# A new order for the first steps of a retention-and-feed-forward kernel: loads, conversions and steps rearranged, some sums tied to program order

## The chip, the cores and the metric

The kernel runs on one core of a Trainium2 chip. The metric is the time of one execution on the device in microseconds (us); lower is better.

## The reference

A retention block is followed by a feed-forward block with a gate. In the first, 4 batches of 8 heads run over 768 positions with 64 channels:

```
state = gamma[h] * state + outer(k[t], v[t])
y[t]  = (1 / sqrt(64)) * q[t] @ state
```

In the second, the heads are laid side by side, so that x has 3072 rows of 512:

```
h   = x @ w_in                            # 512 x 2048
g   = h * (1 / (1 + exp(-1.702 * h)))
out = g @ w_out                           # 2048 x 512
```

All is float32. The two weights reach the kernel as 64-bit numbers, of which it makes 32-bit ones itself.

## The kernel before

**Blocks.** The 3072 rows of x are cut into blocks of 512 (m = 0 to 5). A block is made from four steps; a step (j = 0 to 23) treats 64 positions of two batches for all heads. For a step, q, k and v are loaded (L140), q and k are turned by TensorE into `pt` (turn, L250) and copied out by ACT (turned, L261), TensorE makes the scores `pa` (L289), DVE multiplies them with the mask (masked, L318), and a second half of the step multiplies scores, old state and v (L297, L306, L312). A step's first half is written `stepJ` in the order below and its second half `step-J`; `step1-0` is the first half of 1 with the second half of 0. decay (L272 on ACT, L274 on POOL) weighs k for the state; aged (L357, L359), updated (L366, L368), state (L325) and x (L347, L349) finish a step on ACT, POOL and DVE.

**Weights.** The 16 pairs of weight pieces w0 to w15 come in two loads each (a and b, 512 KB, L180) into three raw buffers used in turn, `RAWS`. The conversion is: abs on ACT (L207), half on DVE (L211, L212, L213), rest on DVE (L217, L218, L222). The pair w0 is converted in two pieces, 0a and 0b.

**Products.** In m = 0 the first layer is plain: `up0.th.p` (L414) takes half the rows (th) and a pair p of weight pieces; `gate` (L393) follows on ACT. In m = 1 the first layer uses seven products for eight (`seven`, L491). From m = 2 on `up` does so (L562), with sums of X (`sums_x`, L530 to L533, on POOL) and of the weights (`sums_w1`). The second layer is `down` for m = 0 and 1 (L799) with sums of gates (`sums_g`, L546 to L548, DVE; `sums_g_late`, L552, POOL) and of w_out (`sums_w2`, L537 to L539; `sums_w2_t3`, L542), and for m = 2 to 5 `down49` (L666), a two-level form which streams weight sums from DRAM through `ring` (`stream`, L635, on POOL) and adds up outputs in `put` (L687 on DVE, L692 to L696 on POOL).

**What sets the order.** TensorE runs in program order. The steps 0 to 7, the conversions and the first layer of blocks 0 and 1 are called from one list of names, written by hand; `pin` (`tc.keep_in_program_order`) holds the instructions of the other engines in that order too, on each engine and each load queue. After the list `ordered` is false, and a scheduler places the instructions that aren't held one by one. Loads are issued from the queues of SP, ACT and POOL, each in its own order.

Of the kernel before, what the change touches and what calls it, by code (L numbers as in the profile page):

```python
# [28 lines left out]
def kernel(  # L29
# [95 lines left out]
    def load(j, what="qkv"):  # L125
# [20 lines left out]
        if j < NEW:  # L146
            if "q" in what:
                plain("q", q, "q_sq", 2)
            if "k" in what:
                plain("kn", k, "k_sq" if j in (0, 1, 4, 5) else "o", 2, pool if j else act)  # L150
# [31 lines left out]
    class Narrow:  # L182
# [26 lines left out]
        def half(self):  # L209
            m, mu, hi = self.m, self.mu, self.hi  # L210
            pin(dve.tensor_scalar(m, m, F64_MOST * 2.0 ** 16, F64_LEAST * 2.0 ** 16, op0=ALU.min, op1=ALU.max))  # L211
            pin(dve.tensor_scalar(mu, mu, 3, None, op0=ALU.logical_shift_left))  # L212
            pin(dve.scalar_tensor_tensor(hi, hi, 0x80000000, mu, op0=ALU.bitwise_and, op1=ALU.bitwise_or))  # L213

        def rest(self):
            m, mu, lo, hi = self.m, self.mu, self.lo, self.hi
            pin(dve.tensor_scalar(mu, hi, 0xFF800000, None, op0=ALU.bitwise_and))  # L217
            pin(dve.scalar_tensor_tensor(lo.bitcast(F32), lo, 2.0 ** -52, m, op0=ALU.mult, op1=ALU.mult))  # L218
            a, b = lo.bitcast(F32), hi.bitcast(F32)
# [42 lines left out]

    def decay(j):
# [5 lines left out]
        if j < NEW:  # L269

            for h in range(H):
                pin(act.activation(KD[j][:, h], x[:, h % HP * 2 + h // HP], AF.Copy, scale=cold[:, H + h:H + h + 1]))  # L272
        else:
            pin(pool.tensor_mul(KD[j].rearrange("p (i s) d -> p i s d", i=2), x.rearrange("p (i s) d -> p i s d", i=2),  # L274
                                cold[:, None, H:H + HP, None].to_broadcast([P, 2, HP, D])))
# [94 lines left out]
    def step(j, f=None):  # L370
        attend(j, f)
        if j is not None:
            masked(j)
            if j > 2 * CB:
                decay(j)
# [145 lines left out]
    def sums_w1(p):  # L521
        t, q1 = w1(p)
        w = [t[:, q1:q1 + 2, s] for s in range(7)]
        pool.tensor_add(w[4], w[2], w[3])
        pool.tensor_sub(w[6], w[0], w[2])
        pool.tensor_sub(w[5], w[4], w[0])
        pool.tensor_sub(w[2], w[1], w[5])

    def sums_x():
        tc.keep_in_program_order(pool.tensor_sub(X[:, 4], X[:, 2], X[:, 0]))  # L530
        pool.tensor_sub(X[:, 6], X[:, 3], X[:, 2])
        pool.tensor_sub(X[:, 5], X[:, 3], X[:, 4])
        pool.tensor_sub(X[:, 2], X[:, 1], X[:, 5])  # L533
# [7 lines left out]
    def sums_w2_t3(p):  # L541
        dve.tensor_sub(W2[:, 6, p:p + 2, :], W2[:, 5, p:p + 2, :], W2[:, 0, p:p + 2, :])  # L542
# [7 lines left out]
    def sums_g_late(m, p):  # L550
        a = [g(m, p, s) for s in range(2)]
        tc.keep_in_program_order(pool.tensor_sub(a[1], a[1], a[0]))  # L552
# [79 lines left out]
    def stream(ring, i):  # L632

        c = ring[:, i % 2 * 3:i % 2 * 3 + 3]
        pool.dma_start(c, W2D[i])  # L635
# [7 lines left out]
    def down49(m, ring, comps):  # L643
# [39 lines left out]
        def put(th, e, half, y, a):  # L683
# [8 lines left out]
            eng.tensor_add(c[:, 1:3], c[:, 1:3], c[:, 0:1].to_broadcast([P, 2, P]))  # L692
            eng.tensor_add(c[:, 3], c[:, 3], c[:, 2])
            eng.tensor_add(c[:, 0:5:4], c[:, 2:4], c[:, 4:5].to_broadcast([P, 2, P]))
            eng.tensor_add(c[:, 2:4], c[:, 0:4:3], c[:, 5:7])
            (act if last else pool).dma_start(rows[th, e], c[:, 1:5].rearrange("p (b f) e -> p b (f e)", b=2))  # L696
# [39 lines left out]
        for i in range(7):  # L736
            for half in range(2):
                def unit(i=i, half=half):
# [11 lines left out]
                    products(acc[x, half], pairs[i][half], i not in (2, 3))  # L750
                    then(i, half, acc[x, half])
                    if half == 0 and i < 6:
                        pairs[i + 1] = derive(i + 1)
                    if half == 1:
                        if i + 2 < 7:
                            comps[i + 2] = stream(ring, i + 2)
# [5 lines left out]
    def down(m):  # L762
# [61 lines left out]
        for n, d in order:  # L824
            key, sa, sb, new, last, then = P_[n]
            def unit(key=key, sa=sa, sb=sb, new=new, last=last, d=d, then=then, n=n):
# [3 lines left out]
                if n == 4 and d == 3:  # L830
# [27 lines left out]

    def rows():
# [9 lines left out]
    def lay_rowd():  # L869

        for o in range(2):
            pin(act.activation(rowd[HALF[o]], products["rows"][HALF[o], o:H:2, :], AF.Copy))

# [11 lines left out]
    def halves_anew():  # L885
# [18 lines left out]
        "warm": keep_warm}  # L904
# [17 lines left out]
    for name, i in [("0a", 0), ("0b", 1)] + [(str(p), 2 * p) for p in range(1, NFF)]:  # L922
        n = Narrow(i)
        works |= {"abs" + name: n.start, "half" + name: n.half, "rest" + name: n.rest}
# [19 lines left out]
    for name in """  # L944
        k0 table q0 warm turn0 w0b rows warm k1 abs0b q1 turned0 step0 v0 w0a half0b mask k2 turn1 causal rest0b
        masked0 decay0 v1 decay1 abs0a half0a step-0 updated0 turned1 q2 step1 rowd whole w2b turn2 w2a x0 k3
        aged1 masked1 turned2 v2 rest0a abs2 q3 step-1 updated1 state1 decay2 aged2 step2 q4 x1 half2 decay3 w3b
        w3a up0.0.0 masked2 turn3 k4 step-2 v3 q5 rest2 k5 gate0.0.0 turned3 updated2 state2 step3 up0.0.2
        masked3 abs3 half3 x2 rest3 turn4 w1b step-3 aged3 gate0.0.2 turned4 state3 w1a w5b updated3 v5 decay4
        abs1 x3 turn5 half1 up0.0.3 turned5 up0.1.2 step4 aged4 w5a rest1 v4 gate0.0.3 decay5 w6a masked4  # L950
        gate0.1.2 abs5 w6b step5-4 half5 rest5 up0.0.1 updated4 abs6 state4 gate0.0.1 w4b
        up0.1.1 half6 aged5 w4a up0.0.5 rest6 masked5 up0.1.5 gate0.1.1 x4 gate0.0.5 abs4 step-5 w8b w8a
        half4 gate0.1.5 state5 updated5 anew q6 up0.1.6 x5 rest4 gate0.1.6 abs8 v6 decay6 aged6 up0.0.6 w7b w7a half8
        turn6 gate0.0.6 up0.1.0 abs7 seven_4.2 seven_6.2 half7 gate0.1.0 w9b w9a up0.1.4 q7 gate0.1.4 step6 masked6 rest7 up0.0.4 v7
        gate0.0.4 seven_52.2 turn7 up0.1.3 gate0.1.3 step7-6 seven_4.0 masked7 updated6 decay7 aged7 abs9 state6 x6 up0.0.7 rest8 seven_w.0 gate0.0.7
# [10 lines left out]
    for m in range(NB):  # L966
# [31 lines left out]
        for n, unit in enumerate(down(m) if m < 2 else down49(m, *ring)):  # L998
# [3 lines left out]
            if m == 0 and NP <= n < 3 * NP // 2:  # L1002
                sums_w2_t3(2 * (n - NP))
            if m == 1 and n % 8 == 3:
                sums_w1(n // 4)
# [4 lines left out]
            if 0 < m < NB - 1 and n == (23 if m == 1 else 11):  # L1010
# [47 lines left out]
```

## Time and profile before

| what | us |
|---|---|
| median of three runs | 661.61 |
| lowest, highest | 657.32, 662.9 |
| the profiled execution | 662.24 |
| its span | 660.5 |
| TensorE busy | 642.2 |
| DVE busy | 453.9 |
| POOL busy | 198.8 |
| ACT busy | 159.0 |

The page gives busy time by engine, and a row of digits for each engine in which one digit stands for the busy tenths of a fortieth of the span, 16.5 us. PE is TensorE, PEld its weight loads, DVE the vector engine, ACT the scalar engine, POOL GpSimd, SP the queue that issues most loads. In the lists of waits a line has the waiting engine with tile and line, the releaser, and then total, number and longest in us. In timelines a line has start, duration, engine, line, operation, output and inputs, and in brackets the idle time before it with what ended it.

### The profile page before, as it was taken

The page shows a single profiled execution, that of the slowest core. Times are in us where ns is not written, and L with a number is a line of the kernel's source. Part 1 is how long each engine was busy: PE and PEld are TensorE (multiplying, and loading weights), DVE is VectorE, ACT ScalarE, POOL GpSimd, SP SyncE. Part 2 cuts the span into 40 slices and gives each one's busy share as a digit, 9 for nine tenths or more (in the row PEclk, how much of TensorE's full clock was granted, in tenths as well). Part 3 has the DMA queues.
Part 4 walks back from the last instruction along what each step waited for, and adds up shares of the span by engine and source line. Part 5 has one row for each costly group of instructions (what it writes and reads, how often), then busy time and mean ns, then how long its engine had stood idle before and what let it go on. Part 6 is the DMA issues. An engine that isn't in the chain of part 4 may idle for free.

```text
span 660.5 us, 15291 instructions
## 1 busy us (share of the span) xinstructions
PE 642.2 (97%) x6390; PEld 580.2 (88%) x6390; DVE 453.9 (69%) x645; ACT 159.0 (24%) x306; POOL 198.8 (30%) x225
## 2 busy tenths in 40 slices
PE   6789999999999999999999999999999999999997
PEld 3778888888788888889999888999888999988997
DVE  3699989999936973556984445995354995254965
ACT  4674233551000000333100233010233110233110
POOL 6400311310379217000536400445600255500000
PEclk9989999999999999999999999999999999999999
DMA  9995549763233556262485832386742252602142
GB/s 176 193 274 173 152 104 241 172 163 60 49 82 135 137 149 153 58 248 96 118 199 134 279 57 97 86 223 135 225 118 97 66 154 104 235 21 96 55 154 96
DMA packets 148149, 91.86 MB, mean 139 GB/s; under 512 B 131600, under 2 KB 134416, under 8 KB 147056
## 3 DMA queue, kind: packets, MB, share of 16 engines
q1 hardware_dynamic: 135856, 45.19, 29.8%
q0 software_dynamic: 9888, 44.46, 20.6%
q10 hardware_dynamic: 2336, 1.25, 0.6%
q8 instruction: 50, 0.82, 0.5%
q14 instruction: 19, 0.16, 0.1%
HBM read 72.89 MB, written 15.47 MB: 134 GB/s over the span
## 4 chain that ended last, share of the span: by engine, by line
PE 89%; DVE 4%; DMA 4%; SPq 1%; issue 1%; ACT 0%; DVEq 0%
PE pq L666 27%; PE px L562 17%; PE pd L799 13%; PE py L562 13%; PE ph L491 7%; PE ph L414 5%; PE pa L289 2%; PE py L312 2%; PE pa L297 2%; PE py L306 2%; DMA W<-in_moe_w_in_dram 1%; DMA W<-in_moe_w_out_dram 1%; DMA q_in<-in_q_dram 1%; PE pt L250 1%; SPq L140 1%
## 5 line engine op out<-in xcount | busy, mean ns | idle before, releaser
L635 POOL DMA_DIRECT2D ring<-W2D x28 | 15.4, 551 | 227.7 <-PE px L562 118.3
L666 PE MATMUL pq<-W,G 128*128 128x128 f32 x672 | 80.2, 276 | 0.0
L666 PEld LDWEIGHTS pq<-W,G 128*128 128x128 f32 x672 | 77.6, 192 | 1.3 <-issue 0.7
L666 PE MATMUL pq<-ring,own 128*128 128x128 f32 x448 | 60.1, 276 | 1.3 <-issue 1.3
L562 PE MATMUL px<-X,W1A 128*128 128x256 f32 x256 | 59.8, 379 | 0.0
L562 PE MATMUL px<-X,W1B 128*128 128x256 f32 x256 | 59.8, 379 | 0.0
L666 PEld LDWEIGHTS pq<-ring,own 128*128 128x128 f32 x448 | 54.5, 192 | 0.4
L562 PEld LDWEIGHTS px<-X,W1B 128*128 128x128 f32 x256 | 48.5, 190 | 6.7
L562 PEld LDWEIGHTS px<-X,W1A 128*128 128x128 f32 x256 | 48.4, 190 | 6.5
L393 ACT ACTIVATE G<-G 128x512 f32<-128x512 f32 x60 | 37.4, 628 | 54.7 <-DVE G L572 33.4
L799 PE MATMUL pd<-W,G 128*128 128x256 f32 x224 | 49.6, 381 | 0.0
L799 PEld LDWEIGHTS pd<-W,G 128*128 128x128 f32 x224 | 42.2, 190 | 5.9
L562 PE MATMUL py<-X,W1A 128*128 128x256 f32 x192 | 45.4, 379 | 0.0
L562 PE MATMUL py<-X,W1B 128*128 128x256 f32 x192 | 45.4, 379 | 0.0
L562 PEld LDWEIGHTS py<-X,W1A 128*128 128x128 f32 x192 | 36.5, 190 | 5.0
L562 PEld LDWEIGHTS py<-X,W1B 128*128 128x128 f32 x192 | 36.5, 190 | 5.0
L580 DVE TENSOR_TENSOR t<-py,u 128x512 f32<-128x512 f32 x16 | 11.1, 692 | 32.3 <-PE py L562 32.3
L569 ACT ACTIVATE p<-px 128x512 f32<-128x512 f32 x16 | 9.6, 597 | 96.0 <-PE px L562 96.0
L414 PE MATMUL ph<-X,W1A 128*128 128x256 f32 x128 | 30.6, 397 | 0.9 <-DVE X L347 0.9
L594 DVE TENSOR_TENSOR G<-G 128x512 f32<-128x512 f32 (+2 forms) x24 | 12.3, 513 | 25.7 <-ACT G L393 25.7
L666 PE MATMUL pq<-ring,G 128*128 128x128 f32 x224 | 29.6, 275 | 0.0
L666 PE MATMUL pq<-W,own 128*128 128x128 f32 x224 | 29.6, 275 | 0.0
(237 smaller groups left out, 1226.0 us busy)
## 6 DMA issues: line engine op xcount, KB each, us to landing
ring<-W2D POOLq DMA_DIRECT2D x28, 768.0 KB, 4.8
W1B<-W1D POOLq DMA_DIRECT2D x6, 1792.0 KB, 9.8
W<-in_moe_w_in_dram SPq DMA_DIRECT2D x12, 512.0 KB, 5.9
W<-in_moe_w_out_dram SPq DMA_DIRECT2D x10, 512.0 KB, 5.8
out_dram<-o POOLq DMA_DIRECT2D x20, 256.0 KB, 3.0
q_sq<-in_q_dram SPq DMA_DIRECT2D x144, 32.0 KB, 2.1
k_sq<-in_k_dram SPq DMA_DIRECT2D x144, 32.0 KB, 2.1
v_in<-in_v_dram SPq DMA_DIRECT2D x72, 64.0 KB, 3.1
```

The lines of the kernel that those rows point to most:

```text
L289: pe.matmul(pa[HALF[w], u, 0, s, :], kt[HALF[u], w, s, :], qt[HALF[u], w, s, :], start=True, stop=True)
L297: pe.matmul(pa[HALF[u], w, 1, s, :], kd[HALF[w], HP * u + s, :], vn[HALF[w], HP * u + s, :], start=True, stop=True)
L306: pe.matmul(py[HALF[o], u, 1, 2 * w + s2, :], old[HALF[u], w, 2 * s2 + o, :], qt[HALF[u], w, 2 * s2 + o, :], start=True, stop=True)
L312: pe.matmul(py[HALF[o], w, 0, 2 * u + s2 if f < NEW else 2 * s2 + u, :], vn[HALF[w], HP * u + s, :], a[HALF[w], u, s, :], start=True, stop ...
L393: pin(act.activation(g, h[:, i], AF.Gelu_apprx_sigmoid))
L414: pe.matmul(h[:, ab], w, X[:, 2 * th + c // 2, c % 2, :], start=(ab == 0 and c == 0), stop=(c == 3), skip_group_check=True)
L491: pe.matmul(acc[:, u, :], w, x, start=(start and u == 0 and c == 0), stop=(stop and c == 1), skip_group_check=True)
L562: pe.matmul(acc[:, u, :], t[:, q1 + u, sa, c, :], X[:, sb, c, :], start=(start and u == 0 and c == 0), stop=(stop and c == 1), skip_group_ ...
L594: dve.tensor_sub(q[0][1], q[0][0], q[0][1])
L635: pool.dma_start(c, W2D[i])
L666: pe.matmul(p0[:, j, :], a[:, d], w[:, d], start=(new and j == 0 and d == 0), stop=(d == NP // 2 - 1), skip_group_check=True)
L799: pe.matmul(p0[:, n, :], g1(m, p, sa)[:, n * P:(n + 1) * P], W2[:, sb, p, :], start=(new and p == 0 and n == 0), stop=(last and p == NP - ...
```

## The change

The list of the first steps is reordered. Within it:

- Step 0's mask is multiplied ahead of half0b; turned1 goes ahead of abs0a; step 1's first and step 0's second half become one call.
- half and rest of some conversions are split (halfa, halfb, resta, restb), with state work in between.
- Small TensorE work that nobody reads is added: `prime` once (28 products) in a free tile and `tick` nine times.
- Three small instructions hold loads back: `hold_w2` (DVE) writes into the raw buffer of w2, `hold_k2` (POOL) reads step 0's masked scores ahead of k2's load, `hold_w1` (ACT) writes into the raw buffer of w1.
- k2 and k3 are loaded from POOL as before, k4 and k5 from SP; decay1 moves from ACT to POOL.
- q7 (with k7) is loaded right behind q6, ahead of w7, and turned before the conversion half7; v6 is behind w7.

Outside the list: `sums_x` moves ahead of the sums of one output piece and is ordered by first use; the decays of steps 16 and 20 come right behind it; the sums of weights and outputs, and the streams, are held in program order; a stream is issued in two pieces and ahead of the output sums; in block 0 `sums_w2_t3` and `sums_g_late` follow the last `sums_g`, the latter on DVE instead of POOL; `sums_w1` comes earlier in block 1.

```diff
-                plain("kn", k, "k_sq" if j in (0, 1, 4, 5) else "o", 2, pool if j else act)
+                plain("kn", k, "k_sq" if j in (0, 1, 4, 5) else "o", 2, (act, pool, pool, pool, sp, sp)[j])
...
-        if j < NEW:
+        if j == 1:
+            pin(pool.tensor_mul(KD[j].rearrange("p (n s) d -> p n s d", n=2), x.rearrange("p (s n) d -> p n s d", n=2),
+                                cold[:, H:2 * H].rearrange("p (n s) -> p n s", n=2)[..., None]
+                                .to_broadcast([P, 2, HP, D])))
+        elif j < NEW:
...
-            if j > 2 * CB:
+            if j in (4 * CB, 5 * CB):
+                last_kd.append(j)
+            elif j > 2 * CB:
                 decay(j)
...
     def sums_x():
         tc.keep_in_program_order(pool.tensor_sub(X[:, 4], X[:, 2], X[:, 0]))
-        pool.tensor_sub(X[:, 6], X[:, 3], X[:, 2])
-        pool.tensor_sub(X[:, 5], X[:, 3], X[:, 4])
-        pool.tensor_sub(X[:, 2], X[:, 1], X[:, 5])
+        tc.keep_in_program_order(pool.tensor_sub(X[:, 5], X[:, 3], X[:, 4]))
+        tc.keep_in_program_order(pool.tensor_sub(X[:, 6], X[:, 3], X[:, 2]))
+        tc.keep_in_program_order(pool.tensor_sub(X[:, 2], X[:, 1], X[:, 5]))
...
-        tc.keep_in_program_order(pool.tensor_sub(a[1], a[1], a[0]))
+        tc.keep_in_program_order((pool if m else dve).tensor_sub(a[1], a[1], a[0]))
...
-        pool.dma_start(c, W2D[i])
+        for k in (slice(1, 2), slice(0, 3, 2)):
+            tc.keep_in_program_order(pool.dma_start(c[:, k], W2D[i][:, k]))
...
+            if (th, e) == (0, 1) and not last:
+                sums_x()
+                while last_kd:
+                    decay(last_kd.pop())
...
                     products(acc[x, half], pairs[i][half], i not in (2, 3))
+                    if half == 1 and i + 2 < 7:
+                        comps[i + 2] = stream(ring, i + 2)
                     then(i, half, acc[x, half])
...
+                    if m == 0 and d == 3:
+                        for p in range(0, NP, 2):
+                            sums_w2_t3(p)
+                        for p in range(0, NP, 2):
+                            sums_g_late(m, p)
...
+    def prime():
+
+        p = ps_a.tile([P, 2, 2, HP, D], F32, name="pa", tag="pa")
+        for s in range(7):
+            for u, w in TWO:
+                pe.matmul(p[HALF[w], u, s // HP, s % HP, :], ident[HALF[u], 0:D], ident[HALF[u], 0:D], start=True, stop=True)
+
+    def hold_w2():
+        pin(dve.memset(RAWS[2][0:1, 0:1], 0))
+
+    def hold_k2():
+        pin(pool.tensor_copy(first, AT[0][:, 0, 0, 0:1]))
+
+    def tick():
+
+        pe.matmul(idle[:, 0:P], ident, ident, start=True, stop=True)
...
+    def hold_w1():
+        pin(act.activation(RAWS[1][0:1, 0:1].bitcast(F32), first[0:1], AF.Copy))
...
-        k0 table q0 warm turn0 w0b rows warm k1 abs0b q1 turned0 step0 v0 w0a half0b mask k2 turn1 causal rest0b
-        masked0 decay0 v1 decay1 abs0a half0a step-0 updated0 turned1 q2 step1 rowd whole w2b turn2 w2a x0 k3
-        aged1 masked1 turned2 v2 rest0a abs2 q3 step-1 updated1 state1 decay2 aged2 step2 q4 x1 half2 decay3 w3b
-        w3a up0.0.0 masked2 turn3 k4 step-2 v3 q5 rest2 k5 gate0.0.0 turned3 updated2 state2 step3 up0.0.2
-        masked3 abs3 half3 x2 rest3 turn4 w1b step-3 aged3 gate0.0.2 turned4 state3 w1a w5b updated3 v5 decay4
-        abs1 x3 turn5 half1 up0.0.3 turned5 up0.1.2 step4 aged4 w5a rest1 v4 gate0.0.3 decay5 w6a masked4
-        gate0.1.2 abs5 w6b step5-4 half5 rest5 up0.0.1 updated4 abs6 state4 gate0.0.1 w4b
-        up0.1.1 half6 aged5 w4a up0.0.5 rest6 masked5 up0.1.5 gate0.1.1 x4 gate0.0.5 abs4 step-5 w8b w8a
-        half4 gate0.1.5 state5 updated5 anew q6 up0.1.6 x5 rest4 gate0.1.6 abs8 v6 decay6 aged6 up0.0.6 w7b w7a half8
-        turn6 gate0.0.6 up0.1.0 abs7 seven_4.2 seven_6.2 half7 gate0.1.0 w9b w9a up0.1.4 q7 gate0.1.4 step6 masked6 rest7 up0.0.4 v7
-        gate0.0.4 seven_52.2 turn7 up0.1.3 gate0.1.3 step7-6 seven_4.0 masked7 updated6 decay7 aged7 abs9 state6 x6 up0.0.7 rest8 seven_w.0 gate0.0.7
+        k0 table q0 warm prime turn0 w0b rows tick tick k1 abs0b q1 mask turned0 step0 v0 half0b hold_w2 causal masked0 turn1 w0a decay0
+        resta0b v1 turned1 whole decay1 hold_k2 k2 w2b w2a tick tick step1-0 masked1 updated0 restb0b q2 abs0a x0 rowd
+        half0a v2 w3b k3 tick tick step-1 resta0a state1 x1 restb0a aged1 updated1 w3a q3 abs2 v3 tick tick tick
+        up0.0.0 gate0.0.0 half2 turn2 turned2 decay2 aged2 decay3 resta2 step2 restb2 masked2 up0.0.2 abs3 gate0.0.2 halfa3
+        turn3 turned3 hold_w1 w1b w1a k4 q4 step-2 updated2 state2 x2 step3 masked3 aged3 halfb3 w5b w5a v4
+        step-3 state3 x3 updated3 resta3 restb3 k5 q5 w6b w6a abs1 up0.1.2 gate0.1.2 up0.1.0 gate0.1.0 half1 v5 turn4 abs5 turned4
+        decay4 up0.0.3 gate0.0.3 rest1 half5 step4 masked4 aged4 up0.0.1 gate0.0.1 w4b w4a turn5 turned5
+        rest5 abs6 up0.1.1 decay5 gate0.1.1 step5-4 half6 masked5 updated4 state4 x4 up0.0.5 aged5 rest6 gate0.0.5
+        up0.1.5 abs4 gate0.1.5
+        step-5 w8b w8a half4 state5 x5 updated5 anew q6 q7 up0.1.6 rest4 gate0.1.6 abs8 w7b w7a v6 decay6 aged6 up0.0.6
+        half8
+        turn6 gate0.0.6 abs7 seven_4.2 seven_6.2 turn7 half7 w9b w9a up0.1.4 gate0.1.4 step6 masked6 rest7 up0.0.4 v7
+        gate0.0.4 seven_52.2 up0.1.3 gate0.1.3 step7-6 seven_4.0 masked7 updated6 decay7 aged7 abs9 state6 x6 up0.0.7 rest8 seven_w.0 gate0.0.7
...
-            if m == 0 and NP <= n < 3 * NP // 2:
-                sums_w2_t3(2 * (n - NP))
-            if m == 1 and n % 8 == 3:
-                sums_w1(n // 4)
+            if m == 1 and n in (0, 3, 5, 7):
+                sums_w1((0, 3, 5, 7).index(n) * 2)
...
-            if 0 < m < NB - 1 and n == (23 if m == 1 else 11):
+            if m == 1 and n == 23:
                 sums_x()
```

## The prediction, as put on record before the result

> **What bounds the kernel now.** I read the page first, then TensorE's waits, then the timeline by engine in the places where TensorE stands idle.
>
> ```profile
> PE 642.2 (97%) x6390; PEld 580.2 (88%) x6390; DVE 453.9 (69%) x645; ACT 159.0 (24%) x306; POOL 198.8 (30%) x225
> PE   6789999999999999999999999999999999999997
> DVE  3699989999936973556984445995354995254965
> DMA  9995549763233556262485832386742252602142
> ```
>
> TensorE is busy in 642.2 of 660.5 us, so 18.3 us is all that waits can give back; 3.6 us of it is the tail after the last matmul. The busy times by stretch give it by place: 7.0 us idle in 0 to 20, 3.5 in 20 to 40, 0.9 in 40 to 60, then only splinters. The waits of TensorE name them:
>
> ```profile
> PE idle L856 <- POOL ident masks.py:199: 3.9, 1, 3.9
> PE pa L289 <- DVE state L366: 2.6, 1, 2.6
> PE pa L289 <- DVE state L368: 1.8, 1, 1.8
> PE pq L666 <- issue: 1.3, 2, 0.7
> PE pd L799 <- DVE W1B L548: 1.2, 2, 0.9
> PE ph L414 <- DVE X L347: 0.9, 1, 0.9
> PE pa L289 <- DVE G L318: 0.9, 1, 0.9
> PE pt L250 <- DMA q_in<-in_q_dram: 0.8, 1, 0.8
> PE pa L289 <- DVE G L253: 0.7, 1, 0.7
> ```
>
> The reader is to see that no wait after 60 us is over 1 us. Busy time hides a second loss, in the timeline of TensorE:
>
> ```profile
> 12.62 1.13 PE L289 MATMUL pa<-G 64*64 64x64 f32 x32
> 36.07 0.69 PE L289 MATMUL pa<-G 64*64 64x64 f32 x32 [1.83 <-DVE state L368]
> 36.70 5.41 PE L414 MATMUL ph<-X,W1A 128*128 128x256 f32 x16
> 78.60 3.62 PE L414 MATMUL ph<-X,W1A 128*128 128x256 f32 x16
> ```
>
> The same 32 instructions take 1.13 us early and 0.69 later, and one up0 took 5.41 where another took 3.62, right after the 1.83 us wait. Granted clock by stretches of 2 us: 0.74, 0.50 and 0.91 from 36 to 42, else 1.00. All of TensorE runs slowly until about 26 us.
>
> Behind the early waits stands ACT, and behind ACT the loads:
>
> ```profile
> 10.08 0.66 ACT L207 ACTIVATE W1A<-W 128x512 f32<-128x512 f32 x1 [4.75 <-DMA W<-in_moe_w_in_dram]
> 17.60 0.66 ACT L207 ACTIVATE W1A<-W 128x512 f32<-128x512 f32 x1 [2.08 <-DMA W<-in_moe_w_in_dram]
> 18.17 1.06 ACT L261 ACTIVATE G<-pt 128x512 f32<-128x512 f32 x2
> 27.75 1.14 ACT L207 ACTIVATE W1A<-G 128x1024 f32<-128x1024 f32 x1 [3.33 <-DMA G<-in_moe_w_in_dram]
> ```
>
> Step 1's turned copy (L261) is ready to run at 15.7 but stands behind abs0a, which waits for w0a until 17.6. DMA engines are full from 4 to 28 us; 203 GB/s is the mean of the first 60.
>
> [...] SP's w0a was issued at 8.59 and ACT could use it only at 17.6; POOL had issued k1 and k2 up to 8.7.
>
> **The change part by part.**
>
> *Start to the first up0.* (a) prime is 28 small matmuls, 56 instructions; at 1.13 us for 32 that is 2.0 us, from 5.9 to 7.9, so turn0 starts 1.2 us later than its 6.75. ACT takes turned0 only after abs0b at 10.7, so this is covered; without that cover it costs 1.2. Nine ticks of 2 instructions (1/4 of a warm's 2.07 us: 0.5 cold, 0.25 warm) lie in waits, 2 to 4 us in all, at a cost of nothing unless the wait they fill has gone. (b) hold_k2 keeps k2 (four transfers of 64 KB) out of the way of w0a: at 200 GB/s it lands 1.3 us earlier, 16.3. hold_k2 itself waits on POOL for masked0 (about 15); behind it stand only k2 and k3, wanted from 25 on. hold_w2 lets w2 go at about 13 instead of 16.6, now ahead of q2: I put it at 24.5 instead of 27.7. (c) turned1 moves ahead of abs0a and decay1 becomes one POOL multiply (1.0 to 1.4 us by the L274 rows) instead of eight ACT copies (2.0 us). (d) The vector engine's stream to the first up0 becomes: mask 0.68, half0b 1.55, masked0 0.69, resta0b 1.45, masked1 0.69, updated0 0.68, restb0b 0.85, half0a 1.55, resta0a 1.11, state1, x1, restb0a 0.69 each: 11.3 us of work by the durations of L211 to L222, L318, L325 and L347. It begins at 10.7 to 11.7 (abs0b; the rows matmul) and I add 1 us of waits for causal (1.85 us on POOL) and for step1-0. So up0.0.0 starts at 23 to 24, taken 23.6, against 28.09. But turn2 and step2 (1.0 + 0.7 us) are no longer done by then.
>
> *First up0 to 55 us.* abs2 follows w2 at 24.5; half2, rest2 take 2.6 + 3.1 us, so up0.0.2 can start at 31.4 (before: 36.70). ACT then owes turned2, decay2, aged2, decay3, abs3 in this order (1.05 + 2.0 + 1.3 + 2.0 + 1.15), so halfa3 starts at 34.2; updated2, state2, x2 and masked3 stand ahead of halfb3 on DVE and wait for step-2, which now comes after up0.0.2 and turn3: 37. From there step3, masked3 (39.5), step-3 (41.1), x3 (42.6), then up0.1.2. At 42.6 TensorE has done what it had done before at 45.4, less turn4 and turn5 (1.9 us): 43.5 before, a gain of 0.9. rest3 slips from 43.8 to about 46.5, but DVE ends rest1 level with before (52.6) and rest5 at about 59.2 instead of 60.1. The wait of 0.9 for masked4 (L318) goes, since step4 has now two conversions' room. Sum: 1.8 us. On SP, w1, k4, q4, w5, k5, q5 stand behind hold_w1, which ACT reaches at 37; w1 lands at 42 and is wanted at 47, w5 at 47 and is wanted at 53: covered by 5 us.
>
> *Clock.* Filling 3.9 to 13 us may bring full clock by 10 to 13 rather than 26; as DVE sets the pace there, this is inside the 23 to 24. On the other side my schedule has TensorE idle for 3 us before up0.0.0 (three ticks fill 0.7), 2.7 us around 30 and 3.2 us between 38 and 43. A cooled window costs 1.7 us as at 38 (5.41 - 3.62, about). One such window was paid before too. Bounds: minus 1.7 (none now) to plus 3.4 (three). I take plus 1.7.
>
> *60 to 182 us.* q7's and k7's sixteen transfers each move ahead of w7 on SP, v6 behind it: about 8 us of q7 issue (0.5 each) against 5 of v6. abs7 was not late and w9, a prefetch, loses its lead. turn7 beside turn6 removes the 0.7 us wait on L253. DVE is the tight engine here: in 60 to 180 its busy time by stretches of 20 sums to 113.6 us, 6.4 idle. In the first down stage it runs without a break:
>
> ```profile
> 171.45 0.68 DVE L542 TENSOR_TENSOR W<-W 128x512 f32<-128x512 f32 x1
> 180.83 1.15 DVE L548 TENSOR_TENSOR W1B<-g,W1B 128x512 f32<-128x512 f32 x1
> ```
>
> Four sums_w2_t3 (0.68) leave the place before the last sums_g and four sums_g_late come from POOL to DVE, all after it: 2.5 us of DVE go from in front of the L548 that TensorE waits 1.2 us for. That wait goes. The 5 us behind it are due only 27 us later.
>
> *182 to 660 us.* TensorE has nothing to win but the two 0.65 us "issue" gaps in L666. Streams are issued ahead of the output sums and in two pieces: 28 more issues of 0.55 us (L635, DMA_DIRECT2D) on a POOL that is 30% busy. What stands behind a pinned stream are output sums, decays and stores; the streams wait up to 33.3 us for TensorE now (118.3 us in 4) and no TensorE wait follows from it, so I cost the pins at nothing. I count half of the gaps, 0.6, bounds 0 and 1.3. sums_x ahead of the output sums and in order of need touches a slack that was not exceeded: nothing.
>
> *Sum.* 1.8 + 0.7 + 1.2 + 0.6 - 1.7 = 2.6 us off the profiled execution's 662.24: 659.6. That execution stands 0.6 over the median of 661.61, so the forecast is 659.0.
>
> **The rivals.** A measurement of this kernel tells about 1% from no change: 655.0 and 668.2 are the bounds.
>
> 1. *Small gain, start only* (the forecast): 652.5 to 665, within 1% mostly. For it: TensorE is at 97% and DVE at 94% in 60 to 182, so an earlier start must be carried by both.
> 2. *The early clock pays off.* If ticks and prime hold full clock from 10 us on and no window cools later, the 1.7 above turns to minus 1.7 (3.4 us), and waits that I put at 30 and 38 to 43 are half as long (3 us more): 659.0 - 6.4 = 652.6. For it: nothing in 10 to 26 us ran at full clock. Against: DVE's 11.3 us.
> 3. *DVE starves behind the fixed order* (slower). Place: DVE and ACT from 24 to 60 us, where halfb3 stands behind x2 and masked3 and all of w1, w5, k4, q5 behind hold_w1. Of DVE's 6.4 idle us until 180 I count 4 as usable; each us by which rest5 ends beyond about 64 comes out at the end. With hold_w1 reached at 48 instead of 37, rest5 ends near 72: 8 us and two more cooled windows: 661.6 + 8 + 3.4 = 673. Against: five us of cover in my schedule.
> 4. *It does nothing*: what is won by 24 us is given back by 60 because step 2 and 3 are merely postponed; 661.
>
> **How the numbers follow.** Case 1 has 0.42, case 4 0.16, case 2 0.18, case 3 0.24. The range reaches to case 2's value and most of case 3: 652.0 to 671.0. Faster by over 1%: case 2 and a little of case 1, 0.2; slower: most of case 3, 0.22; the rest 0.58.
>
> **What would show it.** Right: up0.0.0 starting at 23 to 24 us, up0.0.2 at 31 to 32, the L318, L253 and L548 waits gone, rest5 done by 60, TensorE's first down matmul at 151 to 152 instead of 153.7. Case 2 shows as 32-instruction pa groups of 0.69 us before 15 us and no clock under 1 from 24 to 45. Case 3 shows as DVE waits of several us for ACT L207 or for TensorE between 30 and 60. I am wrong altogether if a new wait on POOL or the ring appears after 182.

## The result, and the profile after

The changed kernel takes 664.46 us (median of 12 runs), the kernel before 659.39 us in the same comparison (12 runs): a ratio of 1.0076, 95% interval 1.0054 to 1.0097, or 5.0 us slower. A small gain of 2.6 us was forecast. Two profiled executions of kernels below lasted two to four times as long as the others (1344 us of `old_start_w1_old`, 2349 us of `new_lean`): neither is read, and the ratios leave them out.

The two profiled executions don't show this difference in full. That of after took 663.20 us and is the fastest of its twelve; that of before took 662.24 us, 2.85 over its median here. Where a few us matter, sizes are therefore taken from ratios below and places from profiles; `before_again` (661.59 us) and `after_again` (664.50 us) are second profiled executions of the two kernels.

First the page of after, busy time and tenths by slice:

```profile
PE 640.9 (97%) x6462; PEld 579.7 (88%) x6462; DVE 459.6 (69%) x650; ACT 157.2 (24%) x299; POOL 207.6 (31%) x243
PE   7779999999999999999999999999999999999997
DVE  3877899999956966456994445995354995254965
DMA  9959478763233446172475832486742352512242
```

TensorE is busier in the first slice (prime and the ticks, 74 of its matmul instructions, compute nothing that is read); the vector engine has its full stretch later. The waits of TensorE in after:

```profile
PE ph L435 <- DVE W1A L235: 2.5, 1, 2.5
PE ph L435 <- DVE X L366: 1.5, 1, 1.5
PE pa L308 <- DVE state L387: 1.4, 1, 1.4
PE pd L827 <- DVE G L569: 1.3, 2, 0.8
...
PE pa L308 <- DVE kT L266: 0.9, 1, 0.9
...
PE py L325 <- DVE X L366: 0.6, 1, 0.6
```

(L435 is up0, L308 to L331 the products of a step, L827 the second layer, L235 the end of a rest, L366 x, L387 updated, L337 masked, L569 the last of sums_g.) The 1.2 us for W1B in the first down stage is gone, and so is the turn's 0.7. New are the waits for L569, for kT and for X: all three lie in the second down stage, after 182 us, where the prediction had TensorE wait for nothing. The start, in the timeline of TensorE:

```profile
23.37 5.38 PE L435 MATMUL ph<-X,W1A 128*128 128x256 f32 x16 [2.47 <-DVE W1A L235]
...
38.58 0.69 PE L308 MATMUL pa<-G 64*64 64x64 f32 x32 [1.38 <-DVE state L387]
40.41 0.69 PE L316 MATMUL pa<-v_in,G 64*64 64x64 f32 x32 [1.14 <-DVE G L337]
...
43.58 6.74 PE L435 MATMUL ph<-X,W1A 128*128 128x256 f32 x30 [1.54 <-DVE X L366]
```

up0.0.0 starts 4.7 us earlier than in the first profile of before, close to the forecast (3.1 us earlier than in the second). Three waits of 1.1 to 1.5 us between 37 and 43.6 us, one after another, then give this back: steps 2 and 3 had only been put off.

Stage marks from the traces (us; the last column is the time from the mark before it, in after less before_again):

| TensorE reaches | before | before_again | after | after_again | stage, after |
|---|---|---|---|---|---|
| first up0 | 28.09 | 26.50 | 23.37 | 22.61 | -3.1 |
| first down product | 153.56 | 152.74 | 153.06 | 154.78 | +3.5 |
| up of block 2 | 261.36 | 260.52 | 263.49 | 264.51 | +2.7 |
| last matmul | 656.93 | 656.36 | 657.91 | 659.17 | -1.4 |

Two stages lose and two gain. The experiments price them.

### The profile page after: what moved, and what is told of

It reads as the page before. It is cut to its first block, busy times and chain, and to the rows that moved or that the text cites. A ratio compares the mean times of both kernels' runs of the same rounds, so it can differ in the third digit from the quotient of the medians.

```text
span 661.5 us, 15491 instructions
## 1 busy us (share of the span) xinstructions
PE 640.9 (97%) x6462; PEld 579.7 (88%) x6462; DVE 459.6 (69%) x650; ACT 157.2 (24%) x299; POOL 207.6 (31%) x243
## 3 DMA queue, kind: packets, MB, share of 16 engines
q0 software_dynamic: 11872, 43.93, 21.3%
q10 hardware_dynamic: 2336, 1.25, 0.6%
## 4 chain that ended last, share of the span: by engine, by line
PE 84%; DVE 8%; DMA 3%; SPq 2%; issue 2%; ACT 1%; ACTq 0%; DVEq 0%
PE pq L688 27%; PE px L583 17%; PE py L583 13%; PE pd L827 9%; PE ph L512 7%; PE ph L435 5%; SPq L157 2%; PE pa L308 2%; DVE X L633 1%; PE py L325 1%; PE py L331 1%; PE pa L316 1%; DMA kn_in<-in_k_dram 1%; DMA W<-in_moe_w_in_dram 1%; DVE G L568 1%
## 5 line engine op out<-in xcount | busy, mean ns | idle before, releaser
L657 POOL DMA_DIRECT2D ring<-W2D x56 | 35.7, 639 | 235.9 <-PE px L583 117.3
L827 PE MATMUL pd<-W,G 128*128 128x256 f32 x224 | 50.6, 383 | 1.5 <-DVE G L569 1.3
L827 PEld LDWEIGHTS pd<-W,G 128*128 128x128 f32 x224 | 41.9, 190 | 8.8 <-DVE G L569 2.2
L435 PE MATMUL ph<-X,W1A 128*128 128x256 f32 x128 | 30.8, 398 | 4.0 <-DVE W1A L235 2.5
L435 PEld LDWEIGHTS ph<-X,W1A 128*128 128x128 f32 x128 | 25.0, 199 | 8.0 <-ACT W1A L207 2.6
```

The source lines that it names most:

```text
L435: pe.matmul(h[:, ab], w, X[:, 2 * th + c // 2, c % 2, :], start=(ab == 0 and c == 0), stop=(c == 3), skip_group_check=True)
L657: tc.keep_in_program_order(pool.dma_start(c[:, k], W2D[i][:, k]))
L827: pe.matmul(p0[:, n, :], g1(m, p, sa)[:, n * P:(n + 1) * P], W2[:, sb, p, :], start=(new and p == 0 and n == 0), stop=(last and p == NP - ...
```

## The experiments

### Which part costs what: the sums of the weights, the list, the rest

`w1_old` is the changed kernel with sums_w1 as before: not pinned, and at its old places in block 1.

```diff
-        tc.keep_in_program_order(pool.tensor_add(w[4], w[2], w[3]))
+        pool.tensor_add(w[4], w[2], w[3])
...
-            if m == 1 and n in (0, 3, 5, 7):
-                sums_w1((0, 3, 5, 7).index(n) * 2)
+            if m == 1 and n % 8 == 3:
+                sums_w1(n // 4)
```

> The changed kernel with one thing undone: the sums of the first layer's weights (sums_w1) are again not held in program order and are placed at the four old points of block 1. Theory A (these sums on GpSimd now run beside the vector engine's gate sums of block 1, which stretch, one of them to 4.70 us, and TensorE loses 4.4 us between 229 and 263 us): this kernel is 3 to 5 us faster than the changed one (664.5), so 659.5 to 661.5, the vector engine's gate sums at 222 to 232 us are 0.7 us each again, and the stage from the first down product of block 0 to the first up product of block 2 shrinks from 110.4 us to about 106. Theory B (the loss is in the first 100 us, where the profiled executions hide it since the one of before was slow and the one of after fast for its kind): the change is under 1 us of the total, and the stage stays near 110.

Measured: 1.0025 [1.0002, 1.0047]. The stage from down to up of block 2 takes 106.02 us instead of 110.43. `order_old` keeps the new sums and goes back to the old list (with k4, k5 and decay1 as they were):

```diff
-        k0 table q0 warm prime turn0 w0b rows tick tick k1 abs0b q1 mask turned0 ...
+        k0 table q0 warm turn0 w0b rows warm k1 abs0b q1 turned0 step0 ...
```

> The changed kernel with the old list of first steps, the old queues for k4 and k5 and decay1 on ACT again; everything outside the list stays changed. Theory A: the first 100 us are worth little, so this is within 1 us of the changed kernel, about 664 to 665. Theory B (the new order costs 3 to 4 us in the usual execution): it is 3 to 4 us faster, about 661.

Measured: 1.0021 [1.0006, 1.0036]. `order_new` is the other way round: the kernel before with the new list, prime, ticks and holds alone.

> The kernel before with the new list of first steps alone (prime, ticks, holds, k4 and k5 on SP, decay1 on GpSimd, q7 early), nothing changed outside it. Theory A: no loss, 658 to 660 beside 659.4 of before. Theory B: slower by 3 to 4 us, 662.5 to 663.5.

Measured: 1.0054 [1.0024, 1.0083]. `old_start_w1_old` undoes both, list and sums, and keeps everything else of the change; `best_again` is the same kernel once more, for its profile.

> Old list of first steps and old place of sums_w1, all else as changed: what is left is the moved sums of w_out and of late gates, sums_x by need, the pins and the streams in two pieces. If the parts add up (1.4 us over before with the list undone, 3.4 of which is sums_w1), it is 2 us faster than before, ratio about 0.997, and beats both kernels. The wait for L569 around 179 us and the ring and X waits after 350 us are absent in its profile. If the loss sits in the pins, it is not faster than before.

> old_start_w1_old once more, for a profile and a second interval: ratio 0.996 to 0.999 again; in the profile the first down product starts at 152.5 to 153.6 us, the stage from there to the first up product of block 2 takes about 106 us (107.8 before), and from there to TensorE's end about 394.7 us (395.6 and 395.8 in the two profiles of before).

Measured: 0.9971 [0.9953, 0.9990] and 0.9959 [0.9939, 0.9979]. This version beats both kernels. `before_again` was run for its profile:

> The kernel before once more, for a second profile. Its first profiled execution took 662.24 against a median of 659.39. Theory B: the second one reaches its first down product (153.6 us in the first profile) 2 to 3 us earlier, by a start without the cooled clock window. Theory A alone: within 1 us of 153.6.

The four combinations agree with each other (the rest of the change is in all four):

| ratio to before | old sums_w1 | new sums_w1 | sums cost |
|---|---|---|---|
| old list | 0.9965 (mean of two) | 1.0021 | 0.0056, 3.7 us |
| new list | 1.0025 | 1.0076 | 0.0051, 3.4 us |
| list costs | 0.0060, 4.0 us | 0.0055, 3.6 us | |

So the moved sums cost some 3.5 us, the new list some 3.8 us, and the rest gives 2.3 us. Each difference of two ratios is uncertain by about 0.003, 2 us; it is the agreement of the two pairs for each cost that makes the sizes firm.

The profiles show where these costs lie. w1_old and best_again differ in the list alone. They reach the first down product at 155.08 and 152.55 us, and from there on take the same time: 106.02 us in both to up of block 2, then 394.82 and 394.79 us to the last matmul. So the list loses ahead of the first down product. The sums lose behind it: with them the stage to up of block 2 takes 110.43 us in after, 109.73 in after_again and 109.39 in order_old.

`order_new` alone has 0.0054, 3.6 us, but this is no third measurement of the list's cost. Its first down product, at 154.34 us, is only 0.8 and 1.6 us later than in the two profiles of before; from up of block 2 to the last matmul it takes 399.00 us, where they take 395.57 and 395.84. The wait behind that is shown below.

**Where the sums lose.** The timeline of DVE in after, then in w1_old, at the same sums of gates:

```profile
220.67 0.68 DVE L567 TENSOR_TENSOR G<-G 128x512 f32<-128x512 f32 x1
221.39 4.70 DVE L568 TENSOR_TENSOR G<-G 128x512 f32<-128x512 f32 x1
226.12 1.66 DVE L569 TENSOR_TENSOR G<-G 128x512 f32<-128x512 f32 x1
227.70 1.52 DVE L567 TENSOR_TENSOR G<-G 128x512 f32<-128x512 f32 x1
```

```profile
222.31 0.68 DVE L567 TENSOR_TENSOR G<-G 128x512 f32<-128x512 f32 x1
223.03 0.69 DVE L568 TENSOR_TENSOR G<-G 128x512 f32<-128x512 f32 x1
```

And POOL in after, where the first line shows why it is late:

```profile
188.75 1.03 POOL L293 TENSOR_TENSOR kd<-kn_in,cold 128x512 f32<-128x512 f32 x1 [19.84 <-PE pd L827]
...
221.82 1.27 POOL L545 TENSOR_TENSOR W1B<-W1B 128x512 f32<-128x512 f32 x1
223.04 1.27 POOL L546 TENSOR_TENSOR W1B<-W1B 128x512 f32<-128x512 f32 x1
224.27 1.26 POOL L547 TENSOR_TENSOR W1B<-W1B 128x512 f32<-128x512 f32 x1
225.61 1.62 POOL L548 TENSOR_TENSOR W1B<-W1B 128x512 f32<-128x512 f32 x1
227.19 1.49 POOL L293 TENSOR_TENSOR kd<-kn_in,cold 128x512 f32<-128x512 f32 x1
```

The reader is to see a vector instruction of 0.69 us that lasts 4.70 us, until 0.56 us after the first three POOL sums have ended, and then 1.66 and 1.52 us beside the fourth and beside the decay behind it. Pinned, the sums stand behind kd of L293, which waits 19.84 us, and then behind output stores, a second kd and a state step; so the last four of sixteen run at 221.8 to 227.2 us instead of ending at 213.0 as in w1_old. There they meet sums_g, which TensorE waits for. In w1_old nothing of this overlaps. w1_old undoes the pin and the place together, so their shares are not shown.

By the profile the DVE sum began 0.43 us ahead of the first POOL sum, and it outlasted three of them (4.70 us against 0.69). By what means the one holds up the other no trace here shows.

The waits for L569 (1.3 us), kT (0.9) and X (0.6) make up 2.8 of the 4.4 us between after and w1_old; in w1_old all three are absent. The wait for L569 comes with the moved sums alone. Waits for kT (0.7) and X (0.6) also stand in this stage of new_fill, a kernel below that has the old sums and takes 108.08 us for it, so these two can have another cause as well. w1_old's stage is 1.8 us shorter than before's 107.8, of which the W1B wait that goes is 1.2.

**What the rest gains.** best_again reaches up of block 2 in 106.02 us from the first down product (before_again: 107.78) and needs 394.79 us from there to the last matmul (before_again: 395.84). That is 1.8 and 1.1 us. Part of the second is sums_x. order_new, which has the old order of sums_x, shows among TensorE's waits

```profile
PE px L581 <- POOL X L551: 3.0, 1, 3.0
```

because L549 and L551 stand on POOL behind kd, which waits 4.76 us for its load, and behind two output sums. The kernel before has the same order and nearly the same waits of kd there (4.39 and 4.70 us in its two profiles). TensorE waits 0.8 us in all for X in before_again and not at all in before. No such wait is left in best_again, where sums_x goes ahead of the output sums and by need.

### What in the list costs: filling, holding, q7

All of these start from w1_old, so 1.0025 is their base. `new_dry` leaves out prime and the nine ticks:

```diff
-        k0 table q0 warm prime turn0 w0b rows tick tick k1 abs0b ...
+        k0 table q0 warm turn0 w0b rows k1 abs0b ...
```

> w1_old (new list, old place of sums_w1; ratio to before 1.0025) without prime and without the nine ticks. Theory C (the spread and loss of the new start is the clock of TensorE, and the filling work helps): slower than w1_old by 1 to 3 us, cooled windows or a cold clock until after 20 us in its profile. Theory D (vector engine and loads set the pace of the start, the clock doesn't matter there): within 0.7 us of w1_old.

Measured: 1.0068 [1.0040, 1.0097], 2.8 us worse, uncertain by some 2.4. The granted clock comes up at 30.2 us; in after it first did at 7.6 (0.50 once more from 11.0 to 14.4). At 21.80 us 27 products of L331 still take 1.11 us (31 take 0.68 in after), and up0.0.0 takes 6.25 us, in after 5.38:

```profile
25.09 6.25 PE L435 MATMUL ph<-X,W1A 128*128 128x256 f32 x16 [2.18 <-DVE W1A L235]
```

The filling is worth its time. More of it shows no gain: `new_fill` has nine ticks ahead of up0.0.0 instead of three.

> w1_old with six more ticks (nine instead of three) in the wait ahead of the first up0. Theory C: faster than w1_old by 0.5 to 1.5 us, since no cooled window falls on the first up0 any more. Theory D: no change, or up to 0.5 us slower where ticks overrun the wait.

Measured: 1.0033 [1.0015, 1.0051]. `new_q7_late` puts q7, w9, v6 and turn7 back to their old places in the list.

> w1_old with the loads of q7 and k7 put back behind w9, v6 back ahead of w7 and turn7 at its old place. Theory F (q7's sixteen q and k loads ahead of w7 on the load queue make abs7 start at 87.5 us instead of 82.6, after 3.9 to 5.7 us of waiting on ACT, and so the conversions behind it late): abs7 starts within 1 us of 83 to 84, and the kernel is 1 to 2 us faster than w1_old, about level with before. Otherwise no change, and 0.7 us lost again on the wait for step 7's turned k.

Measured: 1.0061 [1.0033, 1.0088], the opposite of what I expected. abs7 does start earlier, at 84.8 us. But the wait that moving q7 takes away comes back larger, with the clock at half behind it (1.13 us for 32 products instead of 0.69):

```profile
95.65 1.13 PE L308 MATMUL pa<-G 64*64 64x64 f32 x32 [3.76 <-DVE G L266]
```

q7's loads, behind w9 again, are issued from 81.0 us there and from 78.7 in before, and so in the new list q7 has to go ahead of w7. That costs abs7 some us (it starts at 85.7 and 87.3 in the two executions of after, at 81.7 to 82.6 with the old list), but less than the wait.

Next the hold on w1. In after, the queue of SP stands still for it, and 24 us later DVE waits for abs6. My theory was that the first causes the second:

```profile
29.32 8.99 SPq L180 DMA_DIRECT2D W<-in_moe_w_in_dram  x2
```

```profile
62.40 0.69 DVE L215 TENSOR_SCALAR W1B<-W1B 128x1024 f32<-128x1024 f32 x1 [2.82 <-ACT W1B L207]
```

`new_no_hold` drops `hold_w1`, `new_abs6` drops it and puts abs6 ahead of turned5 on ACT, `new_abs6_hold` does only the latter:

```diff
-        turn3 turned3 hold_w1 w1b w1a k4 q4 ...
+        turn3 turned3 w1b w1a k4 q4 ...
...
-        ... w4b w4a turn5 turned5 rest5 abs6 up0.1.1 ...
+        ... w4b w4a abs6 turn5 turned5 rest5 up0.1.1 ...
```

> w1_old (ratio 1.0025 to before) without hold_w1. Theory G (the load queue stands empty-handed from about 31 to 38 us behind hold_w1, so w5, k5, q5 and w6 come 6 us late: w6 lands at 58.9 to 61.1 us against 52.9 before, rest6 ends at 71.0 against 67.2, and from there the vector engine, which has no slack, is late): w6 lands by 55; rest6 ends 1 to 4 us earlier and the kernel is 1 to 3 us faster than w1_old. If abs6, which stands behind turned5 on ACT, is what makes half6 late: w6 lands early, but half6 still waits 2.8 us, no change in time.

> new_no_hold with abs6 ahead of turned5 on ACT as well. Theory G with abs6: half6 follows rest5 without the 2.8 us wait, rest6 ends at 68 to 69, the waits of TensorE for W1B L235 and G L337 around 93 to 98 us go, 2 to 4 us faster than w1_old, at or below before (ratio 0.996 to 1.000). If the loss of the new start lies in the clock alone: no change from w1_old.

> w1_old with hold_w1 kept and abs6 ahead of turned5. If only the place of abs6 matters: as fast as new_abs6. If the held loads matter: w6 lands at 59 to 61 as before, abs6 waits for it and turned5 behind it, and it is no faster than w1_old or slower by up to 1 us.

Measured: 0.9998 [0.9978, 1.0018], 0.9997 [0.9979, 1.0015] and 1.0013 [0.9989, 1.0037]. Without the hold w6 lands at 53.7 and 55.8 us instead of w1_old's 58.3 and 60.4, but DVE waits for abs6 as long as ever. The line is of new_no_hold:

```profile
65.05 0.69 DVE L215 TENSOR_SCALAR W1B<-W1B 128x1024 f32<-128x1024 f32 x1 [2.81 <-ACT W1B L207]
```

So the theory is refuted: the hold did not cause this wait. What ACT does ahead of abs6 in after is

```profile
59.39 0.60 ACT L414 ACTIVATE W1A<-ph 128x512 f32<-128x512 f32 x1 [2.40 <-PE ph L435]
59.89 0.59 ACT L274 ACTIVATE G<-pt 128x512 f32<-128x512 f32 x1
60.74 0.60 ACT L274 ACTIVATE G<-pt 128x512 f32<-128x512 f32 x1 [0.26 <-PE pt L263]
61.23 1.14 ACT L207 ACTIVATE W1B<-W 128x1024 f32<-128x1024 f32 x1
```

The first is gate0.0.1, which waits for up0.0.1; turned5 and abs6 stand behind it. With abs6 ahead of turned5 the wait is 1.48 us, with and without the hold, and neither time gains clearly by it. In the old list abs6 stands ahead of this gate and starts at 54.69 us (best_again). No run puts it there in the new list. Whether dropping the hold gains is open: 0.0027 from w1_old, 1.8 us, is no more than the uncertainty of such a difference. All three kernels are still above the old list's 0.9965.

### A break that the profile gives no reason for

Six of the eight kernels above that have the new list reached up0.0.0 at 24.3 to 27.6 us rather than at 23.4. Their TensorE stops in the middle of step 1's products. The timeline of TensorE in new_no_hold:

```profile
17.57 0.24 PE L316 MATMUL pa<-v_in,G 64*64 64x64 f32 x1 [0.50 <-DVE state L385]
21.36 1.02 PE L316 MATMUL pa<-v_in,G 64*64 64x64 f32 x28 [3.56 <-issue]
```

One product of this group has run, and "issue" means that nothing in the profile released the others. The DMA view of 12 to 21.3 us of the same kernel has, beside load queues that fill all 16 engines (90% or more in each of its 40 slices), one packet of another kind (queue, kind, then packets, MB and share):

```profile
q8 instruction: 1, 0.02, 0.8%
```

It has 16384 B and runs from 18.70 to 19.92 us. After has 51 such packets in all, and TensorE's records in the trace are 13,078 (6,616 and 6,462): 256 for each packet, which makes 13,056 together. Kernels with 12,911 to 12,970 records have 50 packets, those with 13,060 to 13,190 have 51. So the packets can hold TensorE's program, 256 instructions each, and it can have waited for the next of them. Three kernels test it.

`new_lean` has one wide product (4 instructions) in place of prime's 28 small ones (112), for about the same time; `new_early` has prime's products twice; `no_hold_again` is new_no_hold unchanged.

```diff
-        p = ps_a.tile([P, 2, 2, HP, D], F32, name="pa", tag="pa")
-        for s in range(7):
...
+        keep_warm()
```

```diff
-        for s in range(7):
+        for s in (*range(7), *range(7)):
```

> The order of new_no_hold with prime's 28 small products (112 instructions of TensorE) replaced by one more wide product (4 instructions, about the same 2 us). Theory H (TensorE stands still at its 450th instruction until the instruction packet of 16384 B[...] has got through the full DMA engines): the stop stays at the 450th instruction counted from the start, which now lies about 108 instructions later in the program, in the L325 or L331 products of step 1; the L316 products of step 1 then run without their break of 2.4 to 4.3 us, the packet starts after 15 us, and TensorE goes on 1.3 to 1.6 us after the packet has ended. Ratio to before 0.995 to 1.000. Rival (a semaphore or data of step 1's L316 products is late): the break stays in L316 of step 1 and the ratio stays 0.9998.

> The order of new_no_hold with prime's products written twice (112 more instructions of TensorE, 1.8 us, ahead of turn0). Theory H: the packet [...] has landed by about 15; the 450th instruction lies 112 instructions earlier, in the first products of step 1 (L308, about 15 us), so the break there is under 1.5 us instead of 2.4 to 4.3, and up0.0.0 starts at 23 to 25; a second packet can now come late at the 706th instruction, ahead of up0.0.0. Ratio 0.995 to 1.000. Rival: the break stays at L316 of step 1 with 2.4 us or more, up0.0.0 starts at 26 to 27 and the ratio is 1.000 to 1.003, since turn0 starts 1.8 us later.

> new_no_hold once more, to see how much its start differs between executions. Theory H: the break at the 450th instruction has the length from the dependency to 1.3 to 1.6 us after the packet's end, whatever that is in this execution (0.4 to 4.3 us so far in kernels of the new order). Rival (a fixed wait): 3.6 us again with another time of the packet.

new_lean and after were each run once more for a profile:

> new_lean once more, for a profile of an ordinary execution. Theory H: no break inside step 1's L316 products; TensorE's 450th instruction lies in step 1's L325 or L331 products, and if the packet is late, the break is there and ends 1.3 to 1.9 us after the packet. Rival (data of step 1's L316 products): the break stays in L316.

> The changed kernel once more. Its profiled execution was the fastest of its twelve. Theory H: in a usual execution the packet starts at 16 to 19 us, TensorE stands still at its 450th instruction for 1 to 4 us, up0.0.0 starts at 24 to 27 us, and the stretch from down to up(2) takes about 110.4 us again for the moved sums of weights. Rival (the start costs nothing, all is the sums): up0.0.0 at 23 to 23.5 us as in the first profile.

Measured in the traces (us; the n-th instruction is counted over TensorE's records, the packet is the first of 16384 B):

| kernel | packet starts, ends | 449th, 450th instruction | stop | from packet's end |
|---|---|---|---|---|
| before | 18.28, 19.63 | 25.17, 25.18 | none | |
| best_again | 18.19, 19.14 | 25.48, 25.48 | none | |
| after | 15.58, 17.07 | 18.02, 18.41 | 0.39 | 1.34 |
| after_again | 15.40, 16.80 | 17.33, 18.30 | 0.97 | 1.50 |
| no_hold_again | 15.66, 17.22 | 17.68, 18.68 | 1.00 | 1.46 |
| order_new | 17.82, 18.95 | 19.00, 20.40 | 1.40 | 1.45 |
| w1_old | 17.29, 18.41 | 17.44, 19.86 | 2.42 | 1.45 |
| new_abs6 | 19.76, 21.07 | 18.73, 22.45 | 3.72 | 1.38 |
| new_no_hold | 18.70, 19.92 | 17.60, 21.36 | 3.76 | 1.44 |
| new_abs6_hold | 18.52, 19.80 | 17.04, 21.34 | 4.30 | 1.54 |
| new_fill | 15.58, 17.29 | 18.01, 18.54 | 0.53 | 1.25 |
| new_q7_late | 16.25, 17.73 | 18.26, 19.10 | 0.84 | 1.37 |
| new_dry | 19.05, 20.30 | 20.40, 21.80 | 1.40 | 1.50 |
| new_lean_again | 19.97, 21.39 | 22.32, 22.78 | 0.46 | 1.39 |
| new_early | 11.01, 12.43 | 15.19, 15.19 | none | |

The stop ends 1.25 to 1.54 us after the packet each time. It stays with the number of the instruction and not with the place in the program, which the timelines of new_lean_again and, in the second fence, new_early show:

```profile
21.98 0.55 PE L325 MATMUL py<-G,state 64*64 64x64 f32 x23
22.78 0.35 PE L325 MATMUL py<-G,state 64*64 64x64 f32 x9 [0.24 <-issue]
```

```profile
21.85 0.92 PE L331 MATMUL py<-G,v_in 64*64 64x64 f32 x23 [1.74 <-issue]
```

In new_lean_again step 1's L316 runs through and the stop lies in L325, 108 instructions further on. In new_early the first packet has landed long before, and the stop comes at the 706th instruction, 256 later, 1.88 us after the end of the second packet (18.82 to 19.97). The rival, late data for L316, is refuted.

The same stops are in the kernel before, where the prediction took them for gaps of the ring:

```profile
354.56 0.27 PE L666 MATMUL pq<-ring,own 128*128 128x128 f32 x1 [0.66 <-issue]
458.22 0.27 PE L666 MATMUL pq<-ring,own 128*128 128x128 f32 x1 [0.65 <-issue]
```

These are TensorE's 7106th and 9410th instruction, 26 and 35 times 256 behind the 450th, and they come 1.42 and 1.56 us after the end of the 27th and 36th packet.

So prime and the ticks have a second price. With them TensorE reaches its 450th instruction at 17 to 19 us (20.4 in new_dry, 24 to 25 with the old list), and the packet comes while the loads fill the DMA engines (in after, 90% or more in 39 of the 40 slices of 12 to 21.3 us). When TensorE asks for it no trace shows. Counted from the 194th instruction (256 ahead of the 450th; it comes at about 12 us, in new_dry at 16), the packet starts 3.0 to 7.1 us later, as against 1.0 to 2.2 us with the old list, where that instruction comes at 17 us. What the stop costs in the end is not shown. Between two executions of one kernel it seems to arrive nearly whole: new_no_hold goes on at 21.36 and reaches the first down product at 156.45 us, no_hold_again at 18.68 and 153.99. But after and after_again go on at 18.41 and 18.30 and reach it at 153.06 and 154.78, so other things vary as much; after_again has a stretch of half clock from 40.0 to 46.8 us (its mean clock is 0.991, that of after 0.995).

Neither variant is a remedy: new_lean has 1.0042 [1.0024, 1.0060], new_early 1.0050 [1.0030, 1.0070]; I had expected 0.995 to 1.000 for both. With one wide product the clock came up only at 19.6 us (32 products at 18.03 us took 1.13 us) and in no_hold_again at 9.1 (0.69 us at 11.92). new_lean's stop was short, 0.46 us, and it is still 2.9 us slower than new_no_hold: the early clock is worth more than this stop. In new_early's profiled execution the clock was at half from 21.6 to 28.4, behind the second stop, and 15 of the 16 products of up0.0.0 took 5.14 us. after_again missed its expectation as well: its stop was 0.97 us, and up0.0.0 started at 22.61.

## Why the prediction was wrong

**Right in its places.** up0.0.0 at 23 to 24 (23.37; 22.61 in after_again), up0.0.2 at 31 to 32 (31.05), rest5 done at 59.2 (59.6), w1 used by ACT at about 42 (41.93). The waits on L318 in step 4, on L253 and on L548 went, and the stage of L548 gained the 1.2 us and more (1.8 between best_again and before_again). The clock, taken at a loss of 1.7, was the right kind of term: filling wins, as new_dry (2.8 us slower without it) and new_lean (2.9 with less of it) show, and the clock fell again behind new waits: in after it was 0.67 from 24 to 26 us and 0.50 from 26 to 28, behind the 2.47 us wait for W1A, and up0.0.0 took 5.38 us where up0.0.2 took 3.72.

**Right by luck.** The ring gaps, for which 0.6 us was counted, were not the ring's but TensorE's stops behind an instruction packet (they end 1.42 and 1.56 us after it), and best_again still has one of 0.6 us. About as much was gained all the same (1.1 us), in part at sums_x. There the prediction saw "a slack that was not exceeded"; in before_again it was, by 0.8 us.

**The step that failed first: the sums after 182 us.** "I cost the pins at nothing" lumped sums_w1 with the streams. Its move is in the diff, and the prediction neither lists the sixteen sums with their 1.3 to 1.7 us on POOL nor asks what stands ahead of them once they are pinned: kd, waiting for TensorE, and the output stores. It costs 3.4 to 3.7 us. That a DVE instruction takes longer beside a busy POOL (4.70 us instead of 0.69) was not considered. The sentence that a new wait on POOL after 182 would make the forecast wrong altogether came true in kind: the new wait names DVE, and POOL is what delays it.

**The second: the start was followed to 60 us only.** up0.1.2 was put at 42.6 us, with 43.5 for the same point of the work in before. It came at 43.58 in after and at 42.3 to 47.9 in the kernels with the new list, so the 0.9 us was not there. The causes are three waits on steps 2 and 3 (1.38, 1.14 and 1.54 us; 3.2 together forecast) and the stop at the 450th instruction, of which the prediction had no term. "Covered by 5 us", said of the loads behind hold_w1, is not refuted: dropping the hold took nothing from DVE's wait. But right behind rest5 DVE waits 2.82 us for abs6, because the new order puts abs6 behind gate0.0.1 and turned5 on ACT. "abs7 was not late" fails in the new list: 85.7 and 87.3 us in the two executions of after; new_q7_late shows that q7's place is right all the same. Instead of a gain of 0.8 us (1.8 and 0.7 less 1.7), the list costs 3.6 to 4.0.

**The rivals.** The fourth had the course of the start: what is won by 24 us is given back by 43.6, because steps 2 and 3 are merely postponed. The third had a part of the loss: DVE waiting behind the fixed order. Its place was off (rest5 was not at 72, but at 59.6; the wait comes right behind it), and so were its size and its reason, hold_w1. No rival had the loss in the second down stage.

**What stays open.** The list's 3.8 us are not split to the end. The hold's share is not clear of the uncertainty, and abs6 ahead of gate0.0.1 was not tried. hold_w2, hold_k2, the split conversions and the later steps 2 and 3 have no run of their own. The stop at the 450th instruction differs from one execution to the next (0.39 to 4.30 us), and its mean over after's runs isn't known, since both of its profiled executions have a short one. Why the packet comes later in some executions than in others was not tried.

## What to carry to other kernels

An edit that ties instructions to program order must be priced like a move: write down what now stands ahead of them and what that waits for, and with which engine's work their new time coincides. Before filling an engine's idle time with dummy instructions, count them: here 28 small products took 1.77 us and 112 instructions, the wide one ahead of them 2.08 us and 4, and TensorE stopped at its 450th instruction for up to 4.30 us, until 1.25 to 1.54 us after the end of an instruction packet that came while the loads filled the DMA engines (90% or more). When a gain at the start is forecast, follow each engine and each queue to where its last late result is used, not to where the change ends. And before a wait is put down to a late load, look at what stands ahead of the waiting instruction on its own engine.

## What the runs showed of the hardware

- A DVE sum of two 128x512 tiles took 4.70 us beside three GpSimd sums instead of 0.69. It and the next two DVE sums ended 0.54 to 0.56 us after the end of a GpSimd instruction (at 225.53, 227.23 and 228.68 us).
- TensorE stopped for up to 4.30 us at its 450th instruction while the loads filled the DMA engines (90% or more in each of 40 slices of 12 to 21.3 us in new_no_hold), and went on 1.25 to 1.54 us after the end of an instruction packet (1.88 for a second packet, at the 706th instruction). Such stops, of up to 0.66 us of idle time, also lie in the kernel before, at multiples of 256 instructions behind the 450th. The profile has all of them as "issue", with no releaser.
- 28 small products and nine ticks were worth 2.8 us (uncertain by some 2.4). Two wide products in a row, of about the same length as one and the 28 small ones, left the clock at half until 19.6 us instead of 9.1 (32 products took 1.13 us at 18.03 us, and 0.69 at 11.92), and the kernel was 2.9 us slower.
